# The start of a fused attention and MLP kernel: statistics of token tile 1 on ScalarE, and tiles 0 to 3 normed in another order

## Chip, cores and metric

One core of a Trainium2 chip. The metric is the device time of one execution in microseconds (us), lower is better. Times inside a trace are counted from the start of the span.

## The reference

```python
def reference(A_x, A_wqkv, A_wo, B_x, B_w1, B_b1, B_w2, B_b2):   # S = 2048 tokens, D = 1024, F = 3584
    xn = _layernorm(A_x)                      # no affine part, eps 1e-5
    s = attention(xn, A_wqkv, A_wo)           # 32 heads of 32
    g = silu(mlp(xn, B_w1, B_b1, B_w2, B_b2)) # mlp norms its input a second time
    return A_x + s * g
```

Only the first layernorm is touched. It works on 16 tiles of 128 tokens by 1024 features.

## The kernel before

The kernel is a program of recorded operations. `op(engine, fn, r=, w=)` appends an instruction to that engine's queue, which runs in order, and derives the waits from the names that are read (`r`) and written (`w`). So the order of these calls is the order on each engine.

```python
def stat(tb):                                   # mean and variance of a tile, VectorE
    for c in range(2):
        op("vector", ... e.bn_stats(stats[:, tb, c, :], xt[:, c * 512:(c + 1) * 512]) ...)
    op("vector", ... e.bn_aggr(mv[:, tb, :], stats[:, tb, :, :]...) ...)

def rstd(lo, hi):                               # (var + eps) ** -0.5
    op("vector" if hi <= 2 else "gpsimd", ... e.tensor_scalar(L(0), mv[:, lo:hi, 1], EPS, None, op0=ALU.add) ...)
    op("gpsimd", ... e.tensor_tensor(L(2), L(0), mhalf[:, 0:hi - lo], op=ALU.pow) ...)

def xnorm(tb):                                  # (x - mean) * rstd, bf16, VectorE
    op("vector", ... e.tensor_scalar(xnb[i], xst[...], mv[:, tb, 0:1], lnp[:, 2, tb:tb + 1], op0=ALU.subtract, op1=ALU.mult) ...)

def norm_pair(p):                               # p = 0 .. 7
    lo, hi = 2 * p, 2 * p + 2
    if p == 0:
        stat(0); rstd(0, 1)
        stat(1); rstd(1, 2)
        xnorm(0); xnorm(1)
        stat(2); stat(3); rstd(2, 4)
    else:
        if p < NP - 1: stat(hi)
        for t in (lo, lo + 1):
            xnorm(t)
            if t >= TDMA: transp(t)             # TDMA = 6
        if p + 1 < NP: stat(hi + 1); rstd(hi, hi + 2)
    ...
```

A normed tile has to be transposed. Tiles 0 to 5 go through TensorE (eight matmuls against an identity) and are copied by ScalarE out of PSUM, the memory that takes TensorE's results; tiles 6 to 15 are transposed by a DMA that the sync queue issues. TensorE's own queue is, per pair of tiles: key and query projection of the pair (`pair_kq`, called the first, second, ... projection below), transposes of the next pair while these are on TensorE, value projection (`pair_v`), the first scores. The fifth projection is that of tiles 8 and 9.

The softmax here doesn't subtract the row's maximum and nothing guards it: scores larger than these inputs give would overflow.

## Time and profile before

| | before |
|---|---|
| time, median of the first 3 runs | 1091.75 us (1090.38 to 1092.24) |
| time, median of 6 runs, those beside the changed kernel included | 1090.86 us |
| span of the profiled run | 1088.82 us |
| TensorE busy in the first 49 us | 44.40 us |

TensorE's waits between 1.4 and 49 us (who waits, for whom, us in total, times, longest):

```profile
PE ps L380 <- DVE hT L353: 2.5, 3, 1.4
PE ps L733 <- DVE ident L312: 1.4, 1, 1.4
PE ps L681 <- DMA xnT<-hT: 0.6, 1, 0.6
```

The first line is TensorE waiting for normed tiles, the last is the fifth projection waiting for the transposed tile 9. These two are all that an edit of the norm can win back.

### The profile page before, as it was taken

Reading aid. Unit: us, or ns where it says so; the run is one execution under the profiler, and the core shown is the slowest. Engines: PE = TensorE matmul, PEld = TensorE weight load, DVE = VectorE, ACT = ScalarE, POOL = GpSimd, SP = SyncE. Lnnn points to the kernel's source line nnn. Section 1 sums busy time; section 2 is a strip of 40 time slices with the busy share of each in tenths; the row PEclk is TensorE's granted clock in tenths of the full one; section 3 lists DMA queues with packets and bytes.
Section 4 is the critical chain, followed back from the end, with each engine's and each line's share of the span. In section 5 each row is a group of like instructions: output and inputs, shape, how many; then the busy total and the mean of one; then the engine's idle time right before and its main releaser. Section 6 shows DMA issues by size and latency. Waiting matters only on the chain.

```text
span 1088.8 us, 61814 instructions
## 1 busy us (share of the span) xinstructions
PE 1077.2 (99%) x29156; PEld 701.0 (64%) x29156; DVE 628.4 (58%) x1399; ACT 1041.1 (96%) x1192; POOL 21.7 (2%) x66
## 2 busy tenths in 40 slices
PE   8999999999999999999999999999999999999998
PEld 5766666666666666666666666666666666666665
DVE  8388742477732576642377743378733377635556
ACT  6799998999999999999999999999999999999993
POOL 3400000000000000000000000000000000000000
PEclk9999999999999999999999999999999999999999
DMA  7844356323374223445333264423264333674434
GB/s 246 162 142 135 118 157 164 113 68 110 101 171 120 59 71 107 121 104 146 87 105 99 69 158 120 126 81 110 81 130 120 89 115 110 196 207 105 108 92 124
DMA packets 209336, 131.92 MB, mean 121 GB/s; under 512 B 52538, under 2 KB 200250, under 8 KB 209082
## 3 DMA queue, kind: packets, MB, share of 16 engines
q1 hardware_dynamic: 209082, 127.97, 43.1%
q8 instruction: 228, 3.74, 1.5%
q14 instruction: 26, 0.21, 0.1%
HBM read 104.87 MB, written 12.06 MB: 107 GB/s over the span
## 4 chain that ended last, share of the span: by engine, by line
PE 55%; ACT 42%; DVE 2%; DMA 1%; issue 0%; POOL 0%
ACT P L856 38%; PE ps L389 34%; PE ps L844 9%; PE ps L873 6%; PE ps L876 6%; ACT u L559 4%; DVE stats L325 1%; PE ps L681 1%; PE ps L697 1%; DMA xnT<-hT 1%; DVE hT L353 0%; DMA OT<-in_A_x_dram 0%; ACT thz L603 0%; DVE mv L327 0%; DVE wq L663 0%
## 5 line engine op out<-in xcount | busy, mean ns | idle before, releaser
L856 ACT ACTIVATE P<-ps 128x1024 bf16<-128x1024 f32 x1024 | 968.8, 1085 | 8.7 <-PE ps L844 4.0
L873 PE MATMUL ps<-P,VP 128*32 128x256 bf16 x4096 | 256.5, 273 | 0.0
L876 PE MATMUL ps<-P,ones 128*32 128x256 bf16 x4096 | 256.4, 273 | 0.0
L389 PE MATMUL ps<-hT,war 128*32 128x352 bf16 (+1 forms) x5376 | 225.4, 309 | 0.0
L389 PE MATMUL ps<-yTc,war 128*32 128x352 bf16 (+1 forms) x5376 | 225.3, 309 | 0.0
L844 PE MATMUL ps<-QT,KT 32*128 32x256 bf16 x4096 | 203.4, 273 | 2.8 <-ACT P L856 0.2
L389 PEld LDWEIGHTS ps<-hT,war 128*32 128x32 bf16 x5376 | 127.9, 96 | 74.2 <-issue 25.4
L389 PEld LDWEIGHTS ps<-yTc,war 128*32 128x32 bf16 x5376 | 127.4, 96 | 74.2 <-DVE xb L542 19.0
L844 PEld LDWEIGHTS ps<-QT,KT 32*128 32x128 bf16 x4096 | 60.7, 92 | 114.9 <-issue 60.4
L599 DVE TENSOR_SCALAR zh<-ps,b2h 128x352 f32<-128x352 f32 (+1 forms) x48 | 27.4, 572 | 182.9 <-PE ps L389 182.9
L565 DVE SCALAR_TENSOR_TENSOR hT<-u,xb 128x352 bf16<-128x352 f32 (+1 forms) x168 | 84.4, 509 | 68.4 <-ACT u L559 68.4
L542 DVE TENSOR_SCALAR xb<-ps,b1T 128x352 f32<-128x352 f32 (+1 forms) x168 | 96.2, 572 | 47.8 <-PE ps L389 43.2
L873 PEld LDWEIGHTS ps<-P,VP 128*32 128x32 bf16 x4096 | 109.2, 97 | 20.3 <-issue 1.3
L876 PEld LDWEIGHTS ps<-P,ones 128*32 128x32 bf16 x4096 | 109.4, 97 | 18.7
L389 PE MATMUL ps<-xnT,wq 128*32 128x352 bf16 (+1 forms) x2688 | 112.7, 309 | 0.0
L389 PEld LDWEIGHTS ps<-xnT,wq 128*32 128x32 bf16 x2688 | 63.8, 96 | 37.2 <-DVE xb L542 9.1
L552 DVE SCALAR_TENSOR_TENSOR u<-u,xb 128x352 f32<-128x352 f32 (+1 forms) x168 | 82.4, 508 | 1.9
L548 DVE TENSOR_TENSOR u<-xb 128x352 f32<-128x352 f32 (+1 forms) x168 | 82.4, 507 | 0.7
L559 ACT ACTIVATE u<-u 128x704 f32<-128x704 f32 (+1 forms) x84 | 71.9, 860 | 0.0
L389 PE MATMUL ps<-xnT,OT 128*32 128x352 bf16 (+2 forms) x1568 | 62.9, 306 | 0.2 <-DVE wq L663 0.2
L389 PE MATMUL ps<-wq,xnT 128*32 128x256 bf16 x1536 | 50.8, 274 | 0.0
L389 PEld LDWEIGHTS ps<-xnT,OT 128*32 128x32 bf16 x1568 | 37.9, 96 | 19.7 <-DVE wq L663 7.7
(53 smaller groups left out, 474.6 us busy)
## 6 DMA issues: line engine op xcount, KB each, us to landing
war<-in_B_w_dram SPq DMA_DIRECT2D x336, 256.0 KB, 3.3
wq<-in_A_wqkv_dram SPq DMA_DIRECT2D x36, 128.0 KB, 2.4
OT<-in_A_x_dram SPq DMA_DIRECT2D x16, 256.0 KB, 5.7
xnT<-in_A_x_dram SPq DMA_DIRECT2D x16, 256.0 KB, 3.2
out_dram<-wq SPq DMA_DIRECT2D x15, 256.0 KB, 2.1
y_scratch<-OT SPq DMA_DIRECT2D x14, 256.0 KB, 2.5
gT_scratch<-gst SPq DMA_DIRECT2D x32, 88.0 KB, 3.1
xnT<-in_A_wo_dram SPq DMA_DIRECT2D x8, 256.0 KB, 4.1
```

The costliest lines, as they stand in the source:

```text
L325: op("vector", lambda e, c=c: e.bn_stats(stats[:, tb, c, :], xt[:, c * 512:(c + 1) * 512]), r=[("xst", tb)], w=[("st", tb, c)], c=677.0)
L389: ins = e.matmul(outs(j), lhsT=lhs(j), rhs=rhs, start=start, stop=stop, tile_position=(0, 32 * j), skip_group_check=True)
L542: x0 = op("vector", lambda e: e.tensor_scalar(xb[:, 0:n], bank(bk, 0, n), b1T[:, f:f + 1], None, op0=ALU.add), r=[("b", bk), "b1"], w=[kx] ...
L548: x = op("vector", lambda e: e.tensor_tensor(ub[:, 0:n], xb[:, 0:n], xb[:, 0:n], op=ALU.mult), r=[kx], w=[ku], c=151 + 1.042 * n)
L552: x = op("vector", lambda e: e.scalar_tensor_tensor(ub[:, 0:n], ub[:, 0:n], 1.0 / 0.044715, xb[:, 0:n], op0=ALU.add, op1=ALU.mult), r=[kx, ...
L559: x = op("scalar", lambda e: e.activation(ut[:, :, 0:n], ut[:, :, 0:n], ACT.Tanh, scale=0.7978845608028654 * 0.044715), r=kus, w=kus, c=48 ...
L565: op("vector", lambda e: e.scalar_tensor_tensor(hT[:, fq, 0:n], ut[:, i, 0:n], 1.0, xq[:, 0:n], op0=ALU.add, op1=ALU.mult), r=[kus[i], kq] ...
L599: x0 = op("vector", lambda e: e.tensor_scalar(zh[:, 0:n], bank(bk, 0, n), 0.25, b2h[:, nb:nb + 1], op0=ALU.mult, op1=ALU.add), r=[("b", bk ...
L844: ins = e.matmul(bank(bks[j], kh * 256, (kh + 1) * 256), lhsT=KT[i2][32 * j:32 * j + 32, k0:k0 + 128], rhs=QT[i2][32 * j:32 * j + 32, qb * ...
L856: op("scalar", lambda e, p=p, sl=sl: e.activation(pb[:, 2 * p:2 * p + 2, :, :].rearrange("p a b q -> p (a b q)"), ps[:, sl * 1024:(sl + 1) ...
L873: e.matmul(bankq(ACC, j, 0, QW), lhsT=VP[vp][:, kb, vo + 32 * j:vo + 32 * j + 32], rhs=pb[:, j, kh, :], start=first, stop=False, tile_posi ...
L876: ins = e.matmul(bankq(ACC, j, QW, 2 * QW), lhsT=ones[:, 0:32], rhs=pb[:, j, kh, :], start=False, stop=last, tile_position=(0, 32 * j), sk ...
```

## The change

The intent: ScalarE idles for 6 us at the start while VectorE is saturated, so ScalarE takes tile 1's statistics, tiles 0 and 1 are normed as soon as they can be, and tile 2 is normed before the statistics of tile 4 instead of after.

```diff
         def norm_pair(p):
             if p == 0:
                 stat(0)
                 rstd(0, 1)
-                stat(1)
-                rstd(1, 2)
-                for t in (0, 1):
-                    xnorm(t)
+                stat_scalar(1)
+                xnorm(0)
+                xnorm(1)
                 stat(2)
+                rstd(2, 3)
                 stat(3)
-                rstd(2, 4)
+                xnorm(2)
+                rstd(3, 4)
+            elif p == 1:
+                stat(4)
+                xnorm(3)
+                stat(5)
+                rstd(4, 6)
             else: ...
+        def stat_scalar(tb):
+            op("scalar", activation(xnb[8], xt, Identity, scale=-1.0 / D, accum_out=neg))    # -mean
+            op("scalar", activation(xnb[8], xt, Square, bias=neg, accum_out=sq))             # sum of (x - mean)^2
+            op("scalar", activation(mean, neg, Copy, scale=-1.0))
+            op("gpsimd", tensor_scalar(lnp[:, 0, tb:tb + 1], sq, 1.0 / D, EPS, op0=mult, op1=add))
+            op("gpsimd", tensor_tensor(lnp[:, 2, tb:tb + 1], lnp[:, 0, tb:tb + 1], mhalf[:, 0:1], op=pow))
+            op("gpsimd", tensor_scalar(mv[:, tb, 1:2], sq, 1.0 / D, None, op0=mult))         # variance, for later
```

(`stat_scalar` is cut to its calls, without the names read and written; `...` marks other cuts, here and in the diffs below, where lines are also joined with semicolons. `stat` is also divided into `bn_half` and `bn_merge`, which changes nothing in itself.)

More of the change, by code (lines that the diff above doesn't have):

```diff
@@ L245, in bass_recurrent_scan__mha_block__mixer_channel_mlp__prompt_kernel @@
         lnp = sb("lnp", [128, 8, NT], F32)
+        mneg = sb("mneg", [128, 2], F32)
         mhalf = sb("mhalf", [128, 4], F32)
@@ L320, in turn_bias, with bn_half, bn_merge, stat @@
             op("scalar", lambda e: e.activation(b2h[:], bankb(bk)[:, FB:FB + DC], ACT.Copy, scale=0.5), r=[("b", bk)], w=["b2"], c=200.0)
-        def stat(tb):
-            xt = xst[:, tb * D:(tb + 1) * D]
-            for c in range(2):
-                op("vector", lambda e, c=c: e.bn_stats(stats[:, tb, c, :], xt[:, c * 512:(c + 1) * 512]),
-                   r=[("xst", tb)], w=[("st", tb, c)], c=677.0)
+        def bn_half(tb, c):
+            op("vector", lambda e: e.bn_stats(stats[:, tb, c, :], xst[:, tb * D + c * 512:tb * D + (c + 1) * 512]),
+               r=[("xst", tb)], w=[("st", tb, c)], c=677.0)
+        def bn_merge(tb):
             op("vector", lambda e: e.bn_aggr(mv[:, tb, :], stats[:, tb, :, :].rearrange("p c s -> p (c s)")),
                r=[("st", tb, 0), ("st", tb, 1)], w=[("mv", tb)], c=209.0)
+        def stat(tb):
+            bn_half(tb, 0)
+            bn_half(tb, 1)
+            bn_merge(tb)
         def rstd(lo, hi):
             L = lambda k: lnp[:, k, lo:hi]
-            op("vector" if hi <= 2 else "gpsimd", lambda e: e.tensor_scalar(L(0), mv[:, lo:hi, 1], EPS, None, op0=ALU.add),
+            op("vector" if hi == 1 else "gpsimd", lambda e: e.tensor_scalar(L(0), mv[:, lo:hi, 1], EPS, None, op0=ALU.add),
                r=[("mv", t) for t in range(lo, hi)], w=[("l0", t) for t in range(lo, hi)], c=169.0)
@@ L340, in ycoef @@
             l2k = [("l2", t) for t in range(lo, hi)]
-            mvk = [("mv", t) for t in range(lo, hi)]
+            mvk = [("mv", t) for t in range(lo, hi)] + [("var", 1)] * (b == 0)
             op("gpsimd", lambda e: e.tensor_tensor(L(4), mv[:, lo:hi, 1], L(2), op=ALU.mult), r=mvk + l2k, w=[("l4", b)])
@@ L702, in pair_v @@
                r=[("b", bk)], w=[("VP", 0, 2 * p), ("VP", 0, 2 * p + 1)], c=480.0)
+        def stat_scalar(tb):
+            xt = xst[:, tb * D:(tb + 1) * D]
+            mean, neg, sq = mv[:, tb, 0:1], mneg[:, 0:1], mneg[:, 1:2]
+            op("scalar", lambda e: e.activation(xnb[8], xt, ACT.Identity, scale=-1.0 / D, accum_out=neg), r=[("xst", tb)], w=[("xnb", 8), "mneg"], c=903.0)
+            op("scalar", lambda e: e.activation(xnb[8], xt, ACT.Square, bias=neg, accum_out=sq), r=[("xst", tb), "mneg"], w=[("xnb", 8), "msq"], c=903.0)
+            op("scalar", lambda e: e.activation(mean, neg, ACT.Copy, scale=-1.0), r=["mneg"], w=[("mv", tb)], c=50.0)
+            op("gpsimd", lambda e: e.tensor_scalar(lnp[:, 0, tb:tb + 1], sq, 1.0 / D, EPS, op0=ALU.mult, op1=ALU.add), r=["msq"], w=[("l0", tb)])
+            op("gpsimd", lambda e: e.tensor_tensor(lnp[:, 2, tb:tb + 1], lnp[:, 0, tb:tb + 1], mhalf[:, 0:1], op=ALU.pow), r=[("l0", tb), "mhalf"],
+               w=[("l2", tb)], c=708.0)
+            op("gpsimd", lambda e: e.tensor_scalar(mv[:, tb, 1:2], sq, 1.0 / D, None, op0=ALU.mult), r=["msq"], w=[("var", tb)])
         def norm_pair(p):
```

## The prediction

> **What bounds the kernel now.** I read the page first, for how much of the span the change can touch at all. It edits only the normalisation at the start, so the question is what the rest of the time is made of.
>
> ```profile
> span 1088.8 us, 61814 instructions
> PE 1077.2 (99%) x29156; PEld 701.0 (64%) x29156; DVE 628.4 (58%) x1399; ACT 1041.1 (96%) x1192; POOL 21.7 (2%) x66
> ...
> ACT P L856 38%; PE ps L389 34%; PE ps L844 9%; PE ps L873 6%; PE ps L876 6%; ACT u L559 4%; DVE stats L325 1%; PE ps L681 1%; PE ps L697 1%; DMA xnT<-hT 1%; DVE hT L353 0%; DMA OT<-in_A_x_dram 0%; ACT thz L603 0%; DVE mv L327 0%; DVE wq L663 0%
> ```
>
> TensorE is busy for 99% and ScalarE for 96%; the chain is exponentials and matmuls. Statistics (L325) are 1% of it, the norm itself (L353) rounds to 0%. Busy times by stage put a figure on it: TensorE works 44.40 of the first 49.00 us and 1032.8 of the remaining 1040. Nothing after 49 us can change except by when it begins, so the whole prize is the 4.6 us in which TensorE isn't busy before 49 us; the first 1.4 us of these pass before its first instruction.
>
> Next, the chain of waits in the first 62 us, in order of time, around tile 1:
>
> ```profile
> 6.83 0.16 DVE lnp L332
> 7.00 0.07 issue
> 7.07 0.80 POOL lnp L334
> 7.87 0.03 issue
> 7.89 0.55 DVE hT L353
> 8.44 1.21 DVE stats L325 x2
> ...
> 24.64 0.85 DVE stats L325 x2
> 25.49 5.84 DMA xnT<-hT
> 31.33 0.05 issue
> 31.37 1.92 PE ps L681 x16
> ```
>
> From 3.64 to 25.49 us the chain is VectorE's queue, with one break: the power on GpSimd (L334) for tile 1. It then passes over a transposing transfer to the matmuls at 31.37, and stays on TensorE until it meets the exponentials at 57 us. So an earlier VectorE queue reaches the end only through this one transfer and a TensorE that can start earlier. Third, the timeline of the start, for the pieces that move:
>
> ```profile
> 5.45 0.56 POOL L334 TENSOR_TENSOR lnp<-lnp,mhalf 128x1 f32<-128x1 f32 x1 [4.34 <-DVE lnp L332]
> 7.07 0.79 POOL L334 TENSOR_TENSOR lnp<-lnp,mhalf 128x1 f32<-128x1 f32 x1 [1.06 <-DVE lnp L332]
> 8.16 2.02 ACT L383 ACTIVATE xnT<-ps 128x1024 bf16<-128x1024 bf16 x2 [6.15 <-PE ps L380]
> 13.15 1.07 PE L380 MATMUL ps<-ident,hT 128*128 128x128 bf16 x16 [0.92 <-DVE hT L353]
> 23.30 1.25 ACT L764 ACTIVATE OT<-OT,lnp 128x1024 bf16<-128x1024 bf16 x1
> ```
>
> Tile 1 is normed at 7.89, transposed on TensorE at 8.50, and copied by ScalarE until 10.18; the first projection matmul starts at 10.32, 2.43 us after the norm. TensorE waits again, 0.92 us, for the norms of tiles 2 and 3. Those two and the 0.57 us at 31.37 are the waits that can be gained. ScalarE is idle for 6.15 us before 8.16: room for tile 1's statistics.
>
> **What the Trainium skill says.** (1) "ScalarE: Activation LUTs", section "What ACT_TABLE_LOAD costs": an ACTIVATE takes 186 ns plus 0.833 ns per element, and 93 ns more per pointer operand; a table switch costs 1283 ns and a drain. L764 (1024 elements, two pointers) comes to 1225 by that and took 1250: it agrees. "Table sets: the hidden batching unit" has the cheap functions in every set. Exp, Tanh, Copy and Identity all run here behind one load (1.28 us, ended at 2.00), so I expect no second one for Square. (2) "ScalarE activation tables: per-element evaluation and per-set limits", section "What a function is on this engine": the accumulator output sums into the engine's accumulator. No time for reading it out is given. (3) "SBUF — State Buffer", section "SBUF: two separate sides": GpSimd and a VectorE op in a two-port mode lock each other out. The two powers above agree: 0.56 us beside bn_stats, 0.79 us when the norm of tile 0 (6.90 to 7.44) ran across it. (4) "Perfetto Trace Analysis", section "Optimizing Scalar/DVE Operations": with VectorE saturated, moving work to ScalarE may pay. Between 8.40 and 12.60 us VectorE was busy 4.10 of 4.20, so it is saturated; but the move pays only if the order lets it use the time.
>
> **The change, part by part.** *Removed from VectorE:* two bn_stats, an aggregate and an add of tile 1. They hold it from 5.28 to 6.90, so 1.62 us.
>
> *Added on ScalarE.* Tile 1 lands at 4.2 (the view of transfers: second issue, at about 1.15, 3.1 us to landing). The Identity with accumulator starts at 4.27. From L764 less one pointer operand it lasts 1.25 - 0.09 = 1.16, or 1.07 with an immediate bias; I take 1.11, so 5.38. Reading the accumulator: estimated at 0.2, since ScalarE's smallest instructions in the trace (128x28 and 128x8, L319 and L320) last 0.19 and 0.18; 5.58, and 0.06 for the dependency, 5.64. Square with a pointer bias, 1.16: 6.80; read-out 0.2: 7.00. The mean's copy (0.2) lies beside what follows.
>
> *Added on GpSimd:* 0.05 for the hand-over, a tensor_scalar of 0.22 (L332's time there), 0.08 to the next, and a power, which now has no norm beside it: 0.56. Tile 1's reciprocal deviation is there at 7.91, and its norm starts at **7.94, against 7.89**. The new chain through two dependent passes of 1024 elements is about as long as the old one. Tile 0's norm starts at about 6.05 instead of 6.90, but TensorE and ScalarE only wait for tile 1 after it.
>
> *What VectorE does with the freed 1.62 us:* it waits. Tile 0's norm ends at 6.6; the next in its queue is tile 1's norm at 7.94; the statistics of tile 2 stand behind it. They couldn't have begun much sooner anyway: the transfer of tile 2 lands at 8.11 (issued 2.11):
>
> ```profile
> OT<-in_A_x_dram SPq DMA_DIRECT2D x1, 256.0 KB, 6.0
> ```
>
> They start at 8.41 instead of 8.36. From there VectorE has the same instructions as before, in another order.
>
> *Reordered:* tile 2 is normed before the statistics of tile 4 (bn_stats twice and aggregate: 1.40 us), so it ends at 8.41 + 1.43 + 1.40 + 0.51 = 11.75 instead of 13.09. Its power (0.22 + 0.08 + 0.71 after 10.05) is ready at 11.1, in time. Tile 3's norm stays behind the statistics of tile 4: 11.66 + 1.40 = 13.06 to 13.59, against 13.54. TensorE is in order: tile 2's transposes follow the projection at once (12.2), tile 3's start at 13.65 instead of 13.60. So the value projection, which needs only tiles 0 and 1 but stands behind tile 3's transposes, moves from 14.06 to about 14.15. Its weights land at 13.06 and hold nothing. From tile 5's statistics on, VectorE runs as before, 0.05 later, and the transposing transfer with it.
>
> Sum: +0.05 to +0.1 us at the value projection, the same at 31.37 and at the end; nothing that shows in 1090.
>
> **The rivals.** *A real gain.* If the accumulator read-out costs nothing and the power stays at 0.56, tile 1's norm starts at 7.5; tile 2's landing then sets the limit, 8.13 against 8.36, so the VectorE queue gains at most 0.23 us. If besides that the transfer at 25.49 (5.84 us) lands clear of its wait, TensorE gains the 0.57 at 31.37 too: about 0.8 less, 1091.0. For it: the intent, and 0.92 us of waiting at 13.15. Against it: tile 3's norm keeps its place behind the same work.
> *The ScalarE chain is longer.* Read-outs of 0.3 and slower hand-overs put tile 1 at 8.3, the first projection at 10.75: +0.4, 1092.2. A second table load would add 1.28 more: 1093.5.
> *A new collision.* That transfer took 5.84 us where its neighbours took 2.7 to 2.8, so it depends on what it meets. Shifted by tenths, it may lose its stall or meet a worse one: -0.6 to +1.5.
> *The planner reorders the long stage.* The program decides some VectorE and ScalarE orders from modelled times. A shifted start could change a choice after 49 us: perhaps 0.3% either way. I think it unlikely, since TensorE and ScalarE set the pace of both.
>
> **Range and chances.** Before is 1091.75 (1090.38 to 1092.24), so runs of one kernel differ by more than any part of the change. I predict 1091.8. The range takes the spread of the runs (about 1 each way) and the rivals (-0.8 to +1.7): 1090.0 to 1093.6. 2% is 22 us; all that happens before TensorE's matmuls become dense is less than 5, so both outer chances are 1%.
>
> **What would show it right or wrong.** In the changed profile: one table load; two ACTIVATEs of 1.05 to 1.2 us from 4.27; the norm of tile 1 between 7.7 and 8.3, with VectorE idle for over a microsecond before it; the statistics of tile 2 at 8.2 to 8.8; TensorE without a wait before tile 2's transposes but with one of about 0.8 before tile 3's; the first projection at 10.2 to 10.8, and the value projection within 0.3 of 14.15. I am wrong if tile 3's norm comes much before 13.5, if the wait at 31.37 changes by more than the VectorE queue does, or if work after 49 us takes another time than 1040 us.

## The result

1089.87 us, median of 6 runs (1089.37 to 1091.14), against 1090.86 for the kernel before on the same occasions. The ratio is 0.9991 with a 95% interval of 0.9978 to 1.0004. (Ratios here are the mean time of one kernel's fast runs over that of the other's of the same rounds, so not quite the ratio of the medians.) By the 2% measure it is "same", as forecast, but 0.13 us below the range.

The page after:

```profile
span 1087.7 us, 61820 instructions
PE 1077.0 (99%) x29156; PEld 700.9 (64%) x29156; DVE 627.3 (58%) x1395; ACT 1043.5 (96%) x1197; POOL 22.6 (2%) x70
```

ScalarE has 5 instructions more, VectorE 4 fewer, GpSimd 4 more. Compared one by one in the two traces, the operations of VectorE, ScalarE, GpSimd and the transfers come in the same order after the start, so nothing was replanned. The chain of waits after, in order of time:

```profile
4.22 1.16 ACT hT L713 x2
5.37 0.02 issue
5.40 1.24 ACT hT L714 x2
6.64 0.10 ACT mv L715
6.74 0.18 POOL lnp L716
6.93 0.07 issue
7.00 0.58 POOL lnp L717
7.58 0.03 issue
7.60 0.55 DVE hT L359
...
13.30 0.62 PE ps L386 x8
13.92 1.75 PE ps L703 x16
...
30.50 1.85 PE ps L687 x16
```

Tile 1 now comes over ScalarE and GpSimd, and its norm starts at 7.60. From 13.30 on the chain stays on TensorE until it meets the exponentials at 56.3: VectorE's queue and the transposing transfer, which carried the old one to 31.33, are off it from there. The same events in the timeline, of before and then of after (value projection, and fifth projection):

```profile
14.06 1.91 PE L697 MATMUL ps<-wq,xnT 128*128 128x256 bf16 x16
31.37 1.92 PE L681 MATMUL ps<-xnT,wq 128*128 128x256 bf16 x16 [0.57 <-DMA xnT<-hT]
```

```profile
13.75 1.91 PE L703 MATMUL ps<-wq,xnT 128*128 128x256 bf16 x16
30.43 1.92 PE L687 MATMUL ps<-xnT,wq 128*128 128x256 bf16 x16
```

So 0.31 us are won by the value projection, and 0.63 more by the fifth projection, where a wait is gone: 0.94 in all. From the fifth projection to the end, before takes 1088.82 - 31.37 = 1057.45 and after 1087.68 - 30.43 = 1057.25, nearly alike. TensorE's waits after:

```profile
PE ps L386 <- DVE hT L359: 2.2, 3, 1.0
PE ps L756 <- DVE ident L313: 1.4, 1, 1.4
```

The question is where the 0.63 comes from. The transfer of tile 9 was issued 0.30 us earlier (25.19 instead of 25.49) but also took less time to land. In the views of transfers in a narrow window at its issue, the last column is us to landing; before first, then after:

```profile
xnT<-hT SPq DMA_TRANSPOSE x1, 5.8
```

```profile
xnT<-hT SPq DMA_TRANSPOSE x1, 5.1
```

### The profile page after: what moved, and what is told of

It is laid out like the page before. It is cut to its first block, busy times and chain, and to the rows that moved or that the text cites. A ratio compares the mean times of both kernels' runs of the same rounds, so it can differ in the third digit from the quotient of the medians.

```text
span 1087.7 us, 61820 instructions
## 1 busy us (share of the span) xinstructions
PE 1077.0 (99%) x29156; PEld 700.9 (64%) x29156; DVE 627.3 (58%) x1395; ACT 1043.5 (96%) x1197; POOL 22.6 (2%) x70
## 4 chain that ended last, share of the span: by engine, by line
PE 54%; ACT 44%; DVE 1%; DMA 0%; issue 0%; POOL 0%; SPq 0%
ACT P L879 40%; PE ps L395 32%; PE ps L867 9%; PE ps L896 5%; PE ps L899 5%; ACT u L565 4%; PE ps L703 1%; PE ps L687 1%; ACT thz L609 0%; DVE stats L324 0%; DMA OT<-in_A_x_dram 0%; DVE wq L669 0%; PE ps L386 0%; DVE hT L359 0%; ACT hT L714 0%
```

## The experiments

The transfers view splits off the packets that bring the engines' own instructions: large ones of 16 KB on queue 8, and small ones of 8 KB on queue 14. One of each fell into tile 9's transfer before. The first is the only packet in 0.8 us, from 27.6 to 28.4 (packets, MB, share), though tile 9's transfer, issued at 25.49, had not landed; the second is in the view of 29.9 to 30.3:

```profile
DMA packets 1, 0.02 MB, mean 20 GB/s; under 512 B 0, under 2 KB 0, under 8 KB 0
...
q8 instruction: 1, 0.02, 7.9%
```

```profile
q14 instruction: 1, 0.01, 4.8%
```

After, the first was there too, but the second came only at 33.1, when tile 9 was done. That made **theory A**: 0.3 us by a shorter chain through tile 1, and 0.6 because a fetch of instructions no longer falls into tile 9's transfer, which is a matter of where the engine stands in its program (**theory D**). Rivals: **B**, the 0.6 is an accident of one execution; **C**, the one-by-one norming does it; **E**, the stall has another cause.

All kernels gave correct results. What decides is in the start of each trace, since the times can't resolve 0.1%. Positions are us from the start of the span; the 17th exponential is ScalarE's 17th instruction on the scores:

| kernel | tile 1 normed | value proj. | 8 KB fetch | tile 9 landed | fifth proj. (wait) | from value to fifth proj. | 17th exponential | span |
|---|---|---|---|---|---|---|---|---|
| before | 7.89 | 14.06 | 30.0 | 31.33 | 31.37 (0.57) | 17.31 | 51.06 | 1088.82 |
| before_again | 7.67 | 13.84 | 29.8 | 31.14 | 31.19 (0.61) | 17.35 | 50.87 | 1088.81 |
| order_only | 7.85 | 14.07 | 30.2 | 31.53 | 31.58 (0.76) | 17.51 | 51.26 | 1089.70 |
| dve_pad | 7.66 | 13.83 | 17.9 | 30.23 | 30.50 (0) | 16.67 | 50.19 | 1089.33 |
| after | 7.60 | 13.75 | 33.1 | 30.29 | 30.43 (0) | 16.68 | 50.11 | 1087.68 |
| after_again | 7.55 | 13.71 | 32.9 | 30.28 | 30.38 (0) | 16.67 | 50.06 | 1087.87 |
| after_third | 7.48 | 13.87 | 33.0 | 29.73 | 30.55 (0) | 16.68 | 50.23 | 1088.23 |
| scalar_only | 7.60 | 13.77 | 32.9 | 29.70 | 30.44 (0) | 16.67 | 50.12 | 1089.99 |
| late | 7.96 | 14.11 | 33.3 | 30.26 | 30.79 (0) | 16.68 | 50.47 | 1089.59 |
| pe_pad | 7.58 | 13.81 | 32.9 | 28.32 | 30.74 (0) | 16.93 | 50.42 | 1088.64 |
| split | 7.57 | 13.25 | 33.1 | 29.21 | 29.93 (0) | 16.68 | 49.61 | 1087.81 |
| split_again | 7.55 | 13.36 | 33.2 | 29.29 | 30.04 (0) | 16.68 | 49.72 | 1087.29 |

The seventh column is the clearest: 16.67 or 16.68 wherever TensorE runs through, 17.31 to 17.51 where the 8 KB fetch comes at about 30. The time that tile 9's transfer took to land goes with it: 5.8 to 6.0 us in the three traces in which both fetches fell into it, 4.4 to 5.1 in the six with the 16 KB fetch alone (dve_pad, the changed kernel three times, scalar_only, late), 2.9 in pe_pad, where neither did.

The 0.31 at the value projection is less firm. With the old chain through tile 1 it began at 13.83 to 14.07 (before, before_again, order_only, dve_pad; mean 13.95), with the new one at 13.71 to 13.87 (the changed kernel three times, scalar_only, pe_pad; mean 13.78), so the mean gain is 0.17. The first pair gives 0.31 because tile 0's input landed alike in both (3.62 and 3.63); in before_again and dve_pad it landed at 3.40 and 3.39.

### before_again: the kernel before, unchanged

> The kernel before, unchanged, as a yardstick for what two traces of one program differ by. If the start is fixed by its waits, the first projection matmul comes again at 10.3 (within 0.1), the value projection at 14.06, and tile 9's transposed data lands at 31.3 with a wait of 0.5 to 0.6 at the fifth projection. If tile 9's late landing was an accident of one run, it lands at 28.5 to 30.5 here and that wait is gone. Ratio 1.000.

Ratio 0.9997 (0.9985 to 1.0010). The wait at the fifth projection and tile 9's late landing came again, so they are no accident. The first projection came at 10.10 and the value projection at 13.84, a miss of 0.2: tile 0's input landed at 3.40 instead of 3.62. So positions at the start move by 0.2 between executions, and differences are better taken within one trace.

### after_again and after_third: the changed kernel, unchanged

> The changed kernel, unchanged. Theory A (a shorter chain through tile 1 gives 0.3 us, and 0.6 us come from the transposed tile 9 landing sooner, both by program and not by accident): value projection at 13.75, fifth projection at 30.4 without a wait, span about 1.0 us below the kernel before. Rival B (the 0.6 us is an accident of one execution): tile 9 lands at 31 and the fifth projection waits again, span only 0.3 below.

Ratio 0.9993 (0.9980 to 1.0005). As theory A said, within 0.05 us at each point of the start; with before_again, rival B falls.

> The changed kernel unchanged, on the same chip as the split one. Start as in its two traces: value projection at 13.7 to 13.75, fifth projection at 30.4 without a wait, 17th exponential at 50.1; ratio to before 0.999 to 0.9995. After the 17th exponential, where all kernels run the same order, 1037.5 to 1039.9 us, as in the ten traces so far.

Ratio 1.0000 (0.9988 to 1.0013). No wait at the fifth projection, but the value projection came at 13.87. The expected 13.7 to 13.75 was missed, as were 30.4 (30.55) and a ratio of 0.999 to 0.9995. Here tile 1 was normed at 7.48, earlier than ever, yet tile 2's input landed only at 8.15 (7.67 in the first trace), and its statistics had to wait for it. That is the limit which the prediction's first rival had named. So the 0.3 us shrinks when the input comes late. With before_again it makes a useful pair: the same value projection (13.87 and 13.84), and 0.64 us apart at the fifth (30.55 and 31.19).

### scalar_only and order_only: the two halves of the change

```diff
 # scalar_only, against after: tile 1 on ScalarE, old order of tiles 2 and 3
-                stat(2); rstd(2, 3); stat(3); xnorm(2); rstd(3, 4)
-            elif p == 1:
-                stat(4); xnorm(3); stat(5); rstd(4, 6)
+                stat(2); stat(3); rstd(2, 4)
```

> Tile 1's statistics on ScalarE, but tiles 2 and 3 normed as a pair after the statistics of tile 4, as before. Theory A: tile 1's norm at 7.6 as in the changed kernel, the norms of 2 and 3 at 12.3 and 12.7, the value projection at 13.75 (the whole 0.3), since the one-by-one order leaves tile 3, which is the last to be waited for, where it was. Rival C (the one-by-one norming gives the gain): tile 1's norm at 7.6, but the value projection at 14.0 and no gain.

Ratio 0.9990 (0.9976 to 1.0004). The value projection was at 13.77, the fifth at 30.44: the whole gain without the reordering. Tile 3's norm came at 12.72, tile 2's at 12.29. Its profiled run was long (1089.99) for another reason, told below.

```diff
 # order_only, against before: tile 1 stays on VectorE, new order of tiles 2 and 3
-                stat(2); stat(3); rstd(2, 4)
+                stat(2); rstd(2, 3); stat(3); xnorm(2); rstd(3, 4)
+            elif p == 1:
+                stat(4); xnorm(3); stat(5); rstd(4, 6)
```

> Tile 1's statistics stay on VectorE; tiles 2 and 3 are normed one by one. Theory A: tile 1's norm at 7.9, tile 2's at about 11.2, tile 3's at 13.0, value projection at 14.05 to 14.1, no gain at the start; the span is that of the kernel before unless tile 9's landing moves by itself. Rival C: value projection at 13.8, a gain of 0.3.

Ratio 1.0000 (0.9988 to 1.0013). Value projection at 14.07, the wait at the fifth at 0.76. Tile 2 is normed 1.4 us sooner (11.21) and nothing comes of it, because TensorE's queue holds tile 3's transposes ahead of the value projection, and tile 3 is normed at 13.06. Rival C falls.

### dve_pad: only VectorE's place in its program moved

```diff
 # against before
         op("vector", lambda e: e.memset(ones[:], 1.0), w=["ones"])
+        for i in range(16):
+            op("vector", lambda e, i=i: e.memset(pad[:, i:i + 1], 0.0), w=[("pad", i)], c=90.0)
```

> The kernel before with sixteen one-column memsets on VectorE in the 2.3 us in which it waits for tile 1 of the input; no chain is touched. In four traces the one small instruction transfer (8 KB) near tile 9's transposed transfer came at 29.8 to 30.2 where VectorE had its old number of instructions, and at 32.9 to 33.1 where it had four fewer. Theory D (that fetch is VectorE's, and it costs the second stall of tile 9): here it comes some 7 us earlier, at 21 to 24, tile 9 lands at 30.2 to 30.6 instead of 31.1 to 31.5, the fifth projection waits 0 to 0.1 instead of 0.57; value projection unchanged at 13.8 to 14.1; span 0.5 lower than before's. Rival E (the fetch belongs to another engine, or the stall to something else): still at 30.0, tile 9 at 31.1 to 31.5, same span.

Ratio 0.9999 (0.9985 to 1.0012). The sixteen memsets took 0.26 us of VectorE's idle time; the value projection stayed at 13.83 (before_again: 13.84). The small fetch, in the view of 17.8 to 18.2 us, had moved by 12 us, further than I expected:

```profile
q14 instruction: 1, 0.01, 6.1%
```

and the fifth projection followed without a wait:

```profile
30.50 1.92 PE L684 MATMUL ps<-xnT,wq 128*128 128x256 bf16 x16
```

Against before_again that is 0.69 us sooner, from sixteen instructions that do nothing. Tile 9's transfer, in before_again and then in dve_pad:

```profile
xnT<-hT SPq DMA_TRANSPOSE x1, 5.9
```

```profile
xnT<-hT SPq DMA_TRANSPOSE x1, 5.0
```

This shows theory D and rules out E: the fetch is VectorE's, and where it falls decides the 0.6 us. It is one trace; that the eight traces with four VectorE instructions fewer don't wait there either agrees with it. By what mechanism it holds up the transposing transfer is not shown; the runs show only that they coincide and move together. The expected gain of 0.5 in the span didn't come (1089.33): this run lost it later.

### late: the chain through tile 1 as long as predicted

```diff
 # against after
+            op("scalar", activation(sqb[:], xt[:, 0:64], Identity, scale=0.0, bias=sq))      # carries sq on, 0.35 us
-            op("gpsimd", tensor_scalar(lnp[:, 0, tb:tb + 1], sq, ...))
+            op("gpsimd", tensor_scalar(lnp[:, 0, tb:tb + 1], sqb[:, 0:1], ...))
```

> The changed kernel with one more dependent ScalarE instruction (64 columns) between tile 1's sum of squares and GpSimd, about 0.35 to 0.45 us, so that tile 1's norm starts at 7.95 to 8.05, where I had predicted it. If my prediction erred only in the length of that chain and in tile 9, then: value projection at 14.05 to 14.15, as I predicted and as in the kernel before; tile 9 without the second stall, at 30.6 to 30.7, so the fifth projection at 30.75 to 30.85 with no wait; 0.5 to 0.6 below before at that point. If the early start of tile 1 also decides the stall: the fifth projection at 31.3.

Ratio 0.9998 (0.9985 to 1.0010). Tile 1 was normed at 7.96, the value projection came at 14.11, the fifth at 30.79, all inside what was expected; only tile 9 landed sooner, at 30.26 instead of 30.6 to 30.7. So with the chain as long as predicted, the value projection is where the prediction had it (14.15), and the 0.6 at the fifth is independent of the chain.

### pe_pad: TensorE's place in its program moved

```diff
 # against after: 24 and 8 matmuls of one column in TensorE's waits before the first two sets of transposes
+            if after != 1:
+                m = 24 if after is None else 8
+                op("tensor", lambda e, m=m: tiny(e, m), r=["ident"], w=[("b", 0)], c=("full", m, 64))
```

> The changed kernel with 32 one-column matmuls in TensorE's waits before the first two sets of transposes (24 and 8). They bring TensorE's next 16 KB instruction transfer, seen at 27.4 and 27.6, some 2.5 us forward, to about 25. Theory D, applied to the first stall: tile 9 is no longer held for 2.3 us by it and lands at 28 to 29.5 instead of 30.3 (tile 8 may land later than 26.6 instead). The start of the fifth projection, which does not wait in this kernel, stays at 30.4. Rival: tile 9 still lands at 30.3, and that stall has nothing to do with TensorE's instructions.

Ratio 0.9999 (0.9985 to 1.0013). The 16 KB fetch came at 23.0 instead of 27.6, earlier than the 25 I had reckoned with. Tile 9 landed at 28.32, 2 us sooner. But the fetch now fell into tile 7's transfer, which landed at 26.21 instead of 24.46, and the fourth projection waited for it:

```profile
26.26 1.92 PE L687 MATMUL ps<-xnT,wq 128*128 128x256 bf16 x16 [0.19 <-DMA xnT<-hT]
```

So the first stall goes with TensorE's instructions as the second goes with VectorE's, and it hits whichever tile is under way. My expectation that the fifth projection would stay at 30.4 missed (30.74): 0.2 from that wait, and the rest from a value projection at 13.81, as tile 2's input landed late (8.09).

### split and split_again: a try at a better version

```diff
 # against after
             elif p == 1:
-                stat(4)
+                bn_half(4, 0)
                 xnorm(3)
+                bn_half(4, 1)
+                bn_merge(4)
                 stat(5)
```

> A try at a better version: the changed kernel with tile 3's norm between the two halves of tile 4's statistics. Tile 3's norm starts at 12.1 instead of 12.75 (its power is ready then), its transposes at 12.7, the value projection at 13.15 instead of 13.75 (its weights land at 12.2 to 13.3). TensorE then runs 0.5 to 0.6 earlier until the fifth projection, which could begin at 29.85 but must wait for tile 9 at 30.3 to 30.4: net gain over the changed kernel 0 to 0.1 us. If tile 9 does not hold it, 0.5 to 0.6.

> The split kernel unchanged, for a second trace of its start. In the first, the fifth projection began at 29.93 and the 17th exponential at 49.61 us, 0.5 before the changed kernel's. If that is by program: value projection 13.2 to 13.3, fifth projection at 29.8 to 30.0 without a wait, 17th exponential at 49.5 to 49.7. If tile 9's early landing (29.2) was an accident: a wait at the fifth projection until 30.3. Ratio to before 0.9985 to 0.9995, as far as the later stage lets it show.

Ratios 0.9994 (0.9981 to 1.0007) and 0.9994 (0.9980 to 1.0007); medians 1090.22 and 1089.46. In the one place where TensorE still waited a whole microsecond, for tile 3, it now waits half of one (waits of TensorE between 9 and 49 us, split):

```profile
PE ps L386 <- DVE hT L359: 0.5, 1, 0.5
```

The value projection came at 13.25 and 13.36, the first 0.1 later than expected and the second 0.06 outside its range. I had expected tile 9 to eat that gain. It didn't: with TensorE's program half a microsecond ahead, its 16 KB fetch came at 26.4, into tile 8's transfer (landed at 28.5 and 28.6 instead of 26.6), and tile 9 landed at 29.2 and 29.3. The fifth projection began at 29.93 and 30.04 (expected of the second: 29.8 to 30.0). Against after_third, timed beside split_again and with the same late landing of tile 2, that is 0.51 us sooner; against the two traces of the kernel before 1.15 to 1.44. In the times of whole runs neither can be told from 1.

### What the times show

From the fifth projection to the end, where the kernels do the same work, the twelve traces took 1057.25 to 1059.55 us (span less fifth projection; after 1057.25, before 1057.45, scalar_only 1059.55). Whole runs of one unchanged kernel differ by as much (up to 3.5), so this spread of 2.3 us needs no change to explain it. It is more than twice the effect at the start, so one pair of runs can come out either way. In scalar_only's trace, set against after's, 1.2 us are lost at one spot: TensorE idles 0.9 us in the middle of a matmul group and goes on at 959.47. A piece of weights issued at 953.59 had landed at 959.41, after 5.8 us against a median of 3.3. That this late piece is the cause was not tested.

## Why the prediction was wrong

**What held.** TensorE's busy 99% left under 5 us to win, and the outcome is "same". Nothing after 49 us was replanned. There was one table load, VectorE idled 1.00 us ahead of tile 1's norm, TensorE waited 0.99 before tile 3's transposes and not before tile 2's. order_only and scalar_only confirm that the reordering is worth nothing and why.

**First failed step: "its norm starts at 7.94, against 7.89".** It was 7.60. The terms, beside the trace:

| term | predicted | measured |
|---|---|---|
| start of the first pass | 4.27 | 4.22 |
| first pass, read-out, dependency | 1.11 + 0.20 + 0.06 = 1.37 | 1.18 |
| second pass, read-out, hand-over | 1.16 + 0.20 + 0.05 = 1.41 | 1.32 |
| GpSimd, to the norm's start | 0.22 + 0.08 + 0.56 + 0.03 = 0.89 | 0.88 |

The read-out of the accumulator was mis-sized. The timeline after:

```profile
4.22 1.06 ACT L713 ACTIVATE hT<-OT 128x1024 bf16<-128x1024 bf16 x1 [2.21 <-DMA OT<-in_A_x_dram]
5.18 0.19 ACT L713 ACTIVATION_READ_ACCUMULATOR hT<-OT 128x1 f32 x1
5.40 1.15 ACT L714 ACTIVATE hT<-OT,mneg 128x1024 bf16<-128x1024 bf16 x1
6.45 0.19 ACT L714 ACTIVATION_READ_ACCUMULATOR hT<-OT,mneg 128x1 f32 x1
```

It lasts 0.19, as estimated, but starts 0.10 before its pass ends, so it adds 0.09. Twice 0.10 for that, 0.05 for the first pass being 1.06 (the immediate bias, which I had averaged with the pointer) and 0.05 for its earlier start are 0.30 of the 0.34; the rest is hundredths. It is the first half of the rival "a real gain", with its limit by tile 2's landing; I had asked for a free read-out there, and an overlapped one was nearly that. With the second step below, the whole of that rival came true: it said about 0.8 less, and the first pair of traces has 0.94 at the fifth projection. late puts the 0.36 back and gets the predicted start.

**Second failed step: "the same at 31.37".** I let the transposing transfer move along with VectorE's queue. The prediction saw that it took 5.84 us where others took 2.8 and that it "depends on what it meets", and its third rival had -0.6 as one end; but I left it to chance. The views of transfers held the reason: that of 27 to 28 us, which is among those I asked of the kernel before, lists one instruction packet of 16 KB, and the window of the other, 29 to 30, I hadn't asked for. The diff takes four instructions from VectorE. dve_pad shows that this, and no part of the norm's order, gives the 0.6. One of the prediction's own signs of being wrong came true here: the wait at 31.37 changed by 0.57 while the transfer's issue, at the end of VectorE's queue, moved by 0.30.

**Third: the base.** I added +0.05 to 1091.75, the median of three runs. Six gave 1090.86. So of the miss of 1.93 us (1091.8 to 1089.87), 0.89 is the base, and 1.04 the effect (0.99 less instead of 0.05 more). With the later base the range would have held, so that the time fell 0.13 us outside it and not inside is chance at this spread of runs. The mechanism is wrong either way: the start was 0.94 us shorter, and I had the value projection 0.05 to 0.1 later and the rest unmoved. The times alone can't show it, for the interval of the ratio (-2.4 to +0.4 us) covers my +0.05; the traces of the start do.

**Open.** How a fetch of instructions holds a transposing transfer: in the trace before, no packet of the transfer begins between 27.4 and 27.7, while the 16 KB packet begins only at 27.7. And what causes the 2.3 us of spread after the start.

## What to carry to other kernels

Before moving work to an idle engine, size the new chain term by term, and count overlaps between an instruction and its companion as well as durations. When a transfer takes twice as long as its neighbours, look at every queue in its window before assuming that it moves with the rest; an edit that only changes how many instructions an engine has can shift such a stall by more than the edit itself is worth. For effects of 0.1%, compare positions inside repeated traces, and take the base from more runs than three.

## What the Trainium skill lacked or had wrong

- "ScalarE: Activation LUTs" gives no cost for reading out the accumulator. Here it is an instruction of 0.19 us that starts 0.10 us before the pass ends, so it adds 0.09. The section "What ACT_TABLE_LOAD costs" does say that back-to-back ACTIVATEs overlap by about 93 ns, which is near that 0.10; the prediction used the section and left this out. The same section's 186 ns plus 0.833 ns per element, 1.04 us for 1024 with an immediate bias, agrees with the 1.06 measured, and 93 ns for the pointer with the 1.15 of the second pass.
- No page has it that instruction fetches hold up DMA transposes; it belongs to "Runtime: NRT & Kernel Launch", beside the section "Instruction fetch mechanics", or to "DMA: Bandwidth & Descriptors". Here a fetch of 16 KB for TensorE goes with 1.6 to 1.7 us more for the tile under way (tile 7 took 4.5 us to land instead of 2.9, tile 8 4.3 instead of 2.7), and one of 8 KB for VectorE with 0.7 to 0.9 in the pairs before and after, before_again and dve_pad (tile 9: 5.8 and 5.1, 5.9 and 5.0).
